# Weights of the experts in half pieces beside every second unit, and the row gathers placed behind the last grams

## The chip, the cores and the metric

The kernel runs on one core of one Trainium2 chip. The metric is the device time of one execution in microseconds. A core has the engines PE (TensorE), DVE (VectorE), ACT (ScalarE), POOL (GpSimd) and SP (SyncE); transfers run on 16 DMA engines. SP and POOL issue transfers, each on a queue of its own.

## The reference

Two stages follow each other. The first is a linear attention with a decaying state over 4 batches, 8 heads, 768 steps and a head size of 48. The second assigns each of the 3072 rows that come out (384 wide) to one of 8 experts with room for 384 rows each, by the order of all gate logits, and sends it through that expert's two matrices.

```python
for t in range(S):
    cur = einsum('bhd,bhe->bhde', u * kt, vt)
    y[:, :, t] = einsum('bhd,bhde->bhe', rt, state + cur)
    state = wt[..., None] * state + einsum('bhd,bhe->bhde', kt, vt)
x = y.transpose(0, 2, 1, 3).reshape(3072, 384)
for idx in argsort(-(x @ w_gate).flatten()):
    tok, e = idx // 8, idx % 8
    if assigned[tok] < 0 and counts[e] < 384:
        assigned[tok] = e; counts[e] += 1
for e in range(8):
    out[assigned == e] = maximum(x[assigned == e] @ w1[e], 0) @ w2[e]
```

Everything is float32 outside; w1 is 8 x 384 x 1024 and w2 is 8 x 1024 x 384, some 1.57 MB for each matrix of an expert.

## The kernel before

**Attention.** The steps are cut into 6 chunks of 128, and a chunk of one batch is a unit: 24 units, u = 0 to 23, chunk by chunk. For each unit SP loads r, k, v and w (192 KB each, rows of 192 bytes) into the tiles `kr`, `vv`, `ww`, of which there are two sets, so that a chunk's loads have to wait for the work of two chunks before. PE makes a cumulative sum of log w (`CUM`, tile `cps`), ACT and DVE turn it into factors, `MUL` on DVE scales k and r (`krs`), PE transposes (`T0`, `T1`) and makes the state product (`U`), the products with the state (`IA`), the grams (`G`, into `gps`) and the outputs (`Y0`, `Y1`, into `yps`). POOL makes r times k times u (`RK`, `RKU`) and from its sums the diagonal product (`DG`, tile `mm`), which DVE fills with the masked grams (`MS0`, `MS1`, line 557). The rows of a chunk go to a scratch tensor `x_scratch` in DRAM as bf16, and the gate logits are made beside it.

**Routing.** The first 20 tiles of rows decide early which 256 rows each expert gets in a first block (`Deal.early`, token list `tok1`, line 890). The rest is settled in rounds that run beside the first block, and gives a second block of 128 rows for each expert (`tok2`).

**Experts.** `Experts.block` goes through the experts: POOL gathers 128 rows by the token list (`gather`, line 1076), PE transposes them (line 1087), multiplies with w1 (`up`, line 1117), ACT or DVE take the positive part (`Fhs`), PE multiplies with w2 (`down`, line 1148), and POOL scatters the 128 output rows (line 1168). The first block has two gathers and two scatters for each expert, the second one.

**Weights.** Each matrix is one transfer on POOL's queue (lines 1024 and 1026), float32 in DRAM, bf16 in SBUF, where it takes 768 KB. Experts 0 to 3 have tiles of their own (`w1_0` to `w2_3`, shown as `w`); experts 4 to 7 go into the tiles `kr`, `vv` and `ww` of the last two chunks, once these are no longer used.

**What sets the order.** All operations are entered in a list with an engine, a cost and the operations that they come after. The attention part is laid out by a table of due times (`AT`, with a period of 4500 ns); `Line.merge` then puts everything else into the gaps, with a model of the clocks of all engines, and the instructions are written out in that order. An operation's `after` is a condition of the planner only: what waits at run time is what reads or writes the same data, or what needs the same one of eight semaphores of POOL's transfers. A weight's issue is entered as `Wi` on POOL and its transfer as `Wd` on the planner's DMA line. The first three come after the grams of units 16, 18 and 20 (`LOADS = 16`), and each also after an earlier transfer:

```python
by = [op["G", LOADS + 2 * len(loads)]] if len(loads) < 3 else []
a = line.add("Wi", (e, i), "POOL", 800, fn, after=begun + users + by, prio=-0.9)
begun = [a] if not loads else [a, loads[-1]]
```

POOL carries out its instructions in order, so that a transfer starts when POOL gets to it.

Of the kernel before, what the change touches and what calls it, by code (L numbers as in the profile page):

```python
# [24 lines left out]
F = 1024  # L25
# [645 lines left out]
FIRST = 256  # L671
# [349 lines left out]

def _weight_loads(nc, e, w1sb, w2sb, moe_w1, moe_w2):

    return [lambda: nc.gpsimd.dma_start(
                out=w1sb, in_=moe_w1[e].rearrange("(fc p) f -> p fc f", p=128)),
            lambda: nc.gpsimd.dma_start(
                out=w2sb, in_=moe_w2[e].rearrange("(fc p) d -> p fc d", p=128))]


class Experts:  # L1030
# [242 lines left out]

ROUNDS = N * (E - 1)
OWN = 4
LOADS = 16


def _constants(tc, const):
# [110 lines left out]
@with_exitstack  # L1390
def kernel(
    ctx: ExitStack,
    tc: tile.TileContext,
    r: bass.AP,
    k: bass.AP,
    v: bass.AP,
    w: bass.AP,
    u: bass.AP,
    moe_w_gate: bass.AP,
    moe_w1: bass.AP,  # L1400
    moe_w2: bass.AP,
    out: bass.AP,
):
    nc = tc.nc
    x_dram = nc.dram_tensor("x_scratch", (N, DX), BF16, kind="Internal").ap()

    cp = ctx.enter_context(tc.tile_pool(name="consts", bufs=1))
    keep = ctx.enter_context(tc.tile_pool(name="keep", bufs=1))
    inp = ctx.enter_context(tc.tile_pool(name="inputs", bufs=1))

    def const(name, shape, dtype=FP32):
        return cp.tile(shape, dtype, name=name, tag=name)

    negl = keep.tile([128, NTILE, E], FP32, name="negl", tag="negl")
    tok1 = keep.tile([128, FIRST * E // 128], I32, name="tok1", tag="tok1")
    tok2 = keep.tile([128, NTILE - FIRST * E // 128], I32, name="tok2", tag="tok2")
    a1 = keep.tile([128, NTILE, E], BF16, name="a1", tag="a1")
    flag = keep.tile([1, 1], I32, name="flag", tag="flag")
    q = keep.tile([E, 1], FP32, name="q", tag="q")
    weights = [(keep.tile([128, 3, F], BF16, name=f"w1_{e}", tag=f"w1_{e}"),  # L1420
                keep.tile([128, F // 128, DX], BF16, name=f"w2_{e}", tag=f"w2_{e}"))
               for e in range(OWN)]

    with ExitStack() as work, tc.manual_schedule():
        nc.scalar.preload_act_table_set("natural_log_exp_and_others")
        consts, later = _constants(tc, const)
        sb = work.enter_context(tc.tile_pool(name="work", bufs=1))
        def psum(name):
            return tc.tile_pool(name=name, bufs=1, space=bass.MemoryType.PSUM,
                                side="right" if "_c" in name else "left")  # L1430
        ps = work.enter_context(psum("psum"))
        wide = psum("psum_c")
        pc = wide.__enter__()
        stores = []
        line, ins, (Cps, Tps, Gps, Yps) = _attention(
            tc, inp, sb, ps, pc, r, k, v, w, u, moe_w_gate, x_dram, negl, consts, stores)
        op = line.op
        fixed = line.plan(lambda o: o.u * PERIOD + AT[o.name])
        assert fixed, "the keys lead to a deadlock"
        fixed = [x for x in fixed if x[1].prio is None]  # L1440


        last = NU - 1
        for c in range(NCH - 2, NCH):
            kr, vv, ww = (t[c % 2].bitcast(BF16) for t in ins)
            flat = kr.rearrange("p b x n -> p (b x n)"), vv.rearrange("p b n -> p (b n)"), \
                ww.rearrange("p b n -> p (b n)")
            for a in ((flat[0][:, :3 * F], flat[0][:, 3 * F:]), (flat[1], flat[2])):
                weights.append((a[0].rearrange("p (k f) -> p k f", k=3),
                                a[1].rearrange("p (k d) -> p k d", d=DX)))  # L1450
        loaded, loads = [], []
        begun = []
        for e in range(E):
            users = []
            if e >= OWN:
                c = NCH - 2 + (e - OWN) // 2
                for uu in range(c * B, c * B + B):
                    users += [op[x, uu] for x in ("MUL", "RK", "U", "Y1", "SUB")]
                    if ("WS", uu) in op:
                        users.append(op["WS", uu])  # L1460
            both = []
            for i, fn in enumerate(_weight_loads(nc, e, *weights[e], moe_w1, moe_w2)):
                by = [op["G", LOADS + 2 * len(loads)]] if len(loads) < 3 else []
                a = line.add("Wi", (e, i), "POOL", 800, fn, after=begun + users + by, prio=-0.9)
                begun = [a] if not loads else [a, loads[-1]]
                loads.append(line.add("Wd", (e, i), "DMA", 3500, lambda: None, after=[a],
                                      lag=1900, prio=-0.3))
                both.append(loads[-1])
            loaded.append(both)

        built = []
        for i, (engine, ns, fn) in enumerate(later):
            built = [line.add("X", i, engine, ns, fn, after=built, prio=0.5)]

        line.pools.update(B=4, D=2, FXG=Experts.XG, FXE=Experts.XE, FHS=Experts.HS,
                          FOS=Experts.OS)
        views = {"T": list(Tps), "D": [Yps[:, 0], Yps[:, 1]],
                 "B": [None, None] + Gps}

        def bank(pool, key):  # L1480
            i = line.slot[key]
            if views[pool][i] is None:

                wide.__exit__(None, None, None)
                new = work.enter_context(psum("psum_c2"))
                views[pool][:2] = [new.tile([128, 512], FP32, name=f"cps{x}", tag=f"cps{x}")
                                   for x in range(2)]
            return views[pool][i]
        deal = Deal(nc, line, bank, sb, consts, negl, "D", 20 * 16)
        deal.flag = flag  # L1490
        zero = deal.step("POOL", 200, lambda: nc.gpsimd.memset(a1[:, EARLY:], 0.0))
        deal.prio = -2
        first = deal.early(tok1, a1, op["LF", EARLY - 1], zero, *built)
        deal.prio = -1
        end = deal.round(q, DEPTHS[0], EARLY, deal.early_worst, op["LF", last])
        for depth in DEPTHS[1:]:
            end = deal.round(q, depth, None, (), end)
        second = deal.settle(q, tok2, a1, CAP - FIRST, end)

        ex = Experts(tc, line, bank, sb, consts, x_dram, weights, out, "F")  # L1500

        gets = ex.block(tok1, FIRST, loaded, 0, False, first,
                        *[op["Ls", c * B + B - 1] for c in range(NCH - 1)],
                        apart=lambda: stores[NCH - 1:])
        store = op["Ls", last].fn

        def apart():
            store()
            for got in gets:
                tc.declare_no_dep(stores[-1].ins, got.ins, reason="rows of other units")  # L1510
        op["Ls", last].fn = apart
        ex.block(tok2, CAP - FIRST, loaded, 1000, True, second, op["Ls", last])

        cs, gs, ys = [op["MUL", last]], [op["MS0", last], op["MS1", last]], [op["XB", last]]
        done = line.merge(fixed, {"B": [cs, cs, gs, gs], "D": [ys, ys]})
        assert done, "no order of all operations"
        for _, o in done:
            o.fn()
            o.last = line.last


    more = nc.values_load(flag[0:1, 0:1], min_val=0, max_val=2 * E)
    with tc.If(more > 0):
        tok = keep.tile([128, NTILE], I32, name="tok", tag="tok")
        with ExitStack() as a:
            sb = a.enter_context(tc.tile_pool(name="b_sb", bufs=1))
            ps = a.enter_context(tc.tile_pool(name="b_ps", bufs=1,
                                              space=bass.MemoryType.PSUM))
            line = Direct()
            banks = [ps.tile([128, 512], FP32, name=f"b{i}", tag=f"b{i}") for i in range(6)]  # L1530
            deal = Deal(nc, line, lambda pool, key: banks[line.slot[key]], sb, consts, negl,
                        "E", NTILE * NTILE)
            with tc.For_i(0, ROUNDS):
                deal.round(q, 8)
            deal.settle(q, tok, None, CAP)
        with ExitStack() as a:
            _experts(tc, a, x_dram, weights, out, tok, consts, "gx")
# [30 lines left out]
```

## Time and profile before

| | |
|---|---|
| median of 6 runs | 271.14 us (268.67 to 272.63) |
| profiled execution | 270.35 us, of which the span 268.4 us |
| PE busy | 217.8 us (81% of the span) |
| DVE, ACT, POOL busy | 143.6, 131.3, 148.6 us |
| share of the DMA engines: SP's queue, POOL's queue | 40.3%, 38.1% |
| moved by SP's and POOL's queue | 21.84 and 19.66 MB |
| mean granted clock of PE | 0.932 |

Bytes are counted at the destination, so that a weight counts with its bf16 size. The page gives the busy share in 40 slices of the span, and the chain of waits follows the work that ended last back from the end. A line of a timeline has start and duration in us, the engine, the line of the kernel, the operation, the tile written and those read, and a count; what stands in brackets is the idle time before it and what ended it. "issue" is time in which an engine waited for nothing that the profile shows. A row for a stretch of time has its length, the busy time and count of PE, of PE's weight loads, of DVE, ACT and POOL, and then PE's clock, the DMA share and GB/s. A DMA share can be a little over 1, where packets of one engine overlap.

### The profile page before, as it was taken

The page shows a single profiled execution, that of the slowest core. Times are in us where ns is not written, and L with a number is a line of the kernel's source. Part 1 is how long each engine was busy: PE and PEld are TensorE (multiplying, and loading weights), DVE is VectorE, ACT ScalarE, POOL GpSimd, SP SyncE. Part 2 cuts the span into 40 slices and gives each one's busy share as a digit, 9 for nine tenths or more (in the row PEclk, how much of TensorE's full clock was granted, in tenths as well). Part 3 has the DMA queues.
Part 4 walks back from the last instruction along what each step waited for, and adds up shares of the span by engine and source line. Part 5 has one row for each costly group of instructions (what it writes and reads, how often), then busy time and mean ns, then how long its engine had stood idle before and what let it go on. Part 6 is the DMA issues. An engine that isn't in the chain of part 4 may idle for free.

```text
span 268.4 us, 10437 instructions
## 1 busy us (share of the span) xinstructions
PE 217.8 (81%) x4469; PEld 161.7 (60%) x4469; DVE 143.6 (54%) x440; ACT 131.3 (49%) x248; POOL 148.6 (55%) x180
## 2 busy tenths in 40 slices
PE   2389997989998999776778481999899997968980
PEld 0266875777786677565566370767566875735850
DVE  6747676476675577546178770256555670114440
ACT  2156885675686667565434320355555664412210
POOL 7444685565756558566362548137765647572341
PEclk9999999999999999999689957579999999997995
DMA  7979798588878968979998993968999999232111
GB/s 146 187 140 173 136 178 200 114 174 186 161 153 179 176 126 190 199 144 179 185 203 104 179 180 79 172 150 184 175 221 203 205 195 257 96 104 76 59 64 66
DMA packets 118388, 42.24 MB, mean 157 GB/s; under 512 B 101440, under 2 KB 113728, under 8 KB 118336
## 3 DMA queue, kind: packets, MB, share of 16 engines
q1 hardware_dynamic: 104128, 21.84, 40.3%
q0 software_dynamic: 14208, 19.66, 38.1%
q8 instruction: 37, 0.61, 0.9%
q14 instruction: 15, 0.12, 0.2%
HBM read 46.61 MB, written 7.47 MB: 202 GB/s over the span
## 4 chain that ended last, share of the span: by engine, by line
PE 61%; DMA 9%; issue 9%; DVE 8%; POOL 4%; another core or an unknown queue 3%; SPq 2%; ACT 1%; POOLq 0%; DVEq 0%
PE yps L320 11%; PE tps L478 7%; PE gps L320 6%; PE tps L320 6%; PE cps L1117 6%; PE gps L1148 5%; PE gps L1117 5%; PE cps L320 4%; PE cps L1148 4%; DMA vv<-in_moe_w_dram 4%; DMA kr<-in_r_dram 3%; PE tps L590 2%; DMA u_bc<-in_u_dram 2%; POOL rku L457 2%
## 5 line engine op out<-in xcount | busy, mean ns | idle before, releaser
L466 POOL TENSOR_TENSOR mm<-diag,dd 128x512 f32<-128x512 f32 x24 | 25.2, 1048 | 54.0 <-DVE dd L461 26.4
L484 ACT COPY krT<-tps 112x512 f32<-112x512 f32 x48 | 28.1, 586 | 23.3 <-PE tps L478 20.1
L1168 POOL DMA_INDIRECT out_dram<-Fos,tok x24 | 24.1, 1003 | 24.5 <-DVE Fos L1158 13.7
L1076 POOL DMA_INDIRECT Fxg<-x_scratch,tok x24 | 23.5, 977 | 21.9 <-PE tps L1087 12.7
L557 DVE COPY_PREDICATED mm<-mask,gps 128x256 f32<-128x256 uint8 x48 | 18.7, 441 | 28.5 <-PE gps L320 14.1
L478 PE MATMUL tps<-ident,krs 128*112 128x128 f32 x192 | 31.8, 292 | 1.4 <-ACT row L604 0.8
L320 PE MATMUL cps<-ww,negut 128*128 128x384 f32 x48 | 24.0, 585 | 11.0 <-issue 5.4
L478 PEld LDWEIGHTS tps<-ident,krs 128*112 128x112 f32 x192 | 22.8, 141 | 12.4 <-issue 6.6
L453 POOL TENSOR_TENSOR rku<-kr 128x384 f32<-128x384 f32 x24 | 24.1, 1004 | 7.4 <-DMA kr<-in_r_dram 7.4
L320 PE MATMUL yps<-mm,vv 64*48 64x64 f32 x768 | 19.9, 232 | 9.4 <-DVE mm L557 6.2
L457 POOL TENSOR_TENSOR rku<-rku,u_bc 128x384 f32<-128x384 f32 x24 | 24.1, 1003 | 2.8 <-DMA u_bc<-in_u_dram 2.8
L320 PEld LDWEIGHTS yps<-mm,vv 64*48 64x48 f32 x768 | 14.6, 125 | 17.8 <-DVE mm L557 10.7
L1148 PEld LDWEIGHTS <-Fhs 128*128 128x128 bf16 x192 | 17.8, 100 | 11.9 <-issue 2.9
L578 ACT COPY xf<-yps 128x512 f32<-128x512 f32 x24 | 14.0, 582 | 21.7 <-PE yps L320 21.6
L447 DVE TENSOR_TENSOR krs<-kr,cps 128x768 f32<-128x768 f32 x24 | 22.7, 946 | 2.5 <-ACT cps L442 1.6
L320 PE MATMUL yps<-krT,sm 48*48 48x64 f32 x384 | 21.8, 230 | 1.6 <-issue 1.5
L320 PE MATMUL yps<-krT,st 48*48 48x64 f32 x384 | 21.6, 230 | 0.3 <-issue 0.3
L442 ACT ACTIVATE cps<-cps 128x768 f32<-128x768 f32 x24 | 19.3, 804 | 4.8 <-DVE cps L438 4.8
L1134 ACT ACTIVATE Fhs<-gps 128x512 bf16<-128x512 f32 x20 | 12.0, 598 | 15.5 <-PE gps L1117 9.4
L1117 PEld LDWEIGHTS <-w 128*128 128x128 bf16 x192 | 15.7, 103 | 6.3 <-issue 4.2
L1134 ACT ACTIVATE Fhs<-cps 128x512 bf16<-128x512 f32 x20 | 11.8, 597 | 15.1 <-PE cps L1117 11.6
L320 PE MATMUL gps<-krT 48*64 48x64 f32 x768 | 17.9, 229 | 1.1 <-issue 1.1
(200 smaller groups left out, 468.6 us busy)
## 6 DMA issues: line engine op xcount, KB each, us to landing
w<-in_moe_w_dram POOLq DMA_DIRECT2D x8, 768.0 KB
ww<-in_w_dram SPq DMA_DIRECT2D x24, 192.0 KB, 3.9
kr<-in_k_dram SPq DMA_DIRECT2D x24, 192.0 KB, 3.9
kr<-in_r_dram SPq DMA_DIRECT2D x24, 192.0 KB, 4.1
vv<-in_v_dram SPq DMA_DIRECT2D x24, 192.0 KB, 4.0
kr<-in_moe_w_dram POOLq DMA_DIRECT2D x4, 768.0 KB
x_scratch<-row SPq DMA_DIRECT2D x7, 384.0 KB, 5.2
vv<-in_moe_w_dram POOLq DMA_DIRECT2D x2, 768.0 KB
```

Of the source, the lines that this page charges most:

```text
L320: ln.last = nc.tensor.matmul(*a, **kw)
L447: fn=lambda u=u, kr=kr, b=b: nc.vector.tensor_tensor(out=KR[slot(("kr", u))][:, :, :, :D], in0=kr[:, b].rearrange("t x (h d) -> t x h d", ...
L453: fn=lambda u=u, kr=kr, b=b: nc.gpsimd.tensor_tensor(out=P[slot(("p", u))], in0=kr[:, b, 0, :], in1=kr[:, b, 1, :], op=ALU.mult))
L457: fn=lambda u=u: nc.gpsimd.tensor_tensor(out=P[slot(("p", u))], in0=P[slot(("p", u))], in1=u_bc, op=ALU.mult))
L466: fn=lambda u=u: nc.gpsimd.tensor_tensor(out=M[slot(("m", u))], in0=_free(diag, [0, 2], [0, NPAIR], [1, 64]), in1=_free(Dg[slot(("dg", u)) ...
L478: ln.last = nc.tensor.transpose(t[:112, at:at + 128], pair_of(s[:, x], j), ident)
L484: nc.scalar.copy(out=KRT[slot(("krt", u))][:112, 2 * half:2 * half + 2].rearrange("p j x t -> p (j x t)"), in_=Tps[slot(("t", u, half))][: ...
L1076: got = nc.gpsimd.indirect_dma_start(out=self.xg[slot[xg[1]]], out_offset=None, in_=self.x_dram, in_offset=bass.IndirectOffsetOnAxis(ap=to ...
L1117: nc.tensor.matmul(self.bank("B", b[1])[:, i * size:(i + 1) * size], lhsT=w1sb[:, k, f8 * 128:(f8 + 1) * 128], rhs=xv()[:, k], start=(k == ...
L1134: nc.scalar.activation(out=to, in_=of, func=AF.Relu)
L1148: nc.tensor.matmul(self.bank("B", b[1])[:, :DX], lhsT=hv()[:, f8, h * 128:(h + 1) * 128], rhs=w2sb[:, f8, :], start=(f8 == 0), stop=(f8 == ...
L1168: put = nc.gpsimd.indirect_dma_start(out=self.out, out_offset=bass.IndirectOffsetOnAxis(ap=tok[:, j:j + 1], axis=0), in_=self.os[slot[o[1] ...
```

## The change

Each matrix is now brought in two halves: w1 by its columns, w2 by its blocks of rows. There are 32 issues of 384 KB on POOL's queue in place of 16 of 768 KB. The n-th comes after the grams of unit 4 + 2n, at most of unit 23 (`LOADS = 4`); from the eleventh on it also comes after the transfer of three before it. An expert's multiplications come after the second half of its matrix in the planner. The gathers of the first block get one more condition in the planner, the grams of the last unit. After these edits the planner lays out all operations anew; up to the logits of the last chunk the order on PE is the same as before.

```diff
 def _weight_loads(nc, e, w1sb, w2sb, moe_w1, moe_w2):
-    return [lambda: nc.gpsimd.dma_start(
-                out=w1sb, in_=moe_w1[e].rearrange("(fc p) f -> p fc f", p=128)),
-            lambda: nc.gpsimd.dma_start(
-                out=w2sb, in_=moe_w2[e].rearrange("(fc p) d -> p fc d", p=128))]
+    w1 = moe_w1[e].rearrange("(fc p) f -> p fc f", p=128)
+    w2 = moe_w2[e].rearrange("(fc p) d -> p fc d", p=128)
+    f, k = F // 2, F // 256
+    return [lambda to=to, of=of: nc.gpsimd.dma_start(out=to, in_=of)
+            for to, of in ((w1sb[:, :, :f], w1[:, :, :f]), (w1sb[:, :, f:], w1[:, :, f:]),
+                           (w2sb[:, :k], w2[:, :k]), (w2sb[:, k:], w2[:, k:]))]
...
-LOADS = 16
+LOADS = 4
...
             for i, fn in enumerate(_weight_loads(nc, e, *weights[e], moe_w1, moe_w2)):
-                by = [op["G", LOADS + 2 * len(loads)]] if len(loads) < 3 else []
+                n = len(loads)
+                by = [op["G", min(LOADS + 2 * n, last)]]
                 a = line.add("Wi", (e, i), "POOL", 800, fn, after=begun + users + by, prio=-0.9)
-                begun = [a] if not loads else [a, loads[-1]]
-                loads.append(line.add("Wd", (e, i), "DMA", 3500, lambda: None, after=[a],
+                begun = [a] if LOADS + 2 * n < last else [a, loads[n - 2]]
+                loads.append(line.add("Wd", (e, i), "DMA", 1750, lambda: None, after=[a],
                                       lag=1900, prio=-0.3))
-                both.append(loads[-1])
+                both += [loads[-1]] * (i % 2)
             loaded.append(both)
...
-        gets = ex.block(tok1, FIRST, loaded, 0, False, first,
+        gets = ex.block(tok1, FIRST, loaded, 0, False, first, op["G", last],
                         *[op["Ls", c * B + B - 1] for c in range(NCH - 1)],
                         apart=lambda: stores[NCH - 1:])
```

## The prediction

> **What bounds the kernel now.** I read the page first, then the chain of waits, then the timelines of PE and POOL, then stretches of time. The page's second part shows two stages with different limits.
>
> ```profile
> PE   2389997989998999776778481999899997968980
> ...
> PEclk9999999999999999999689957579999999997995
> DMA  7979798588878968979998993968999999232111
> ```
>
> A slice is 6.71 us. Up to slice 15 PE is nearly full and the DMA engines are at about 0.8. From slice 16 on (107 us) the DMA share goes to 0.9 and more while PE falls to 0.4 to 0.8. From slice 28 to 33 both are full, and then the DMA falls quiet and PE alone works to the end. The chain names what was late at the three seams:
>
> ```profile
> 127.17 8.96 DMA kr<-in_r_dram
> ...
> 159.65 7.93 another core or an unknown queue
> ...
> 212.24 11.34 DMA vv<-in_moe_w_dram
> ```
>
> The first is an input load of unit 22 that landed 9 us after its issue, the second a wait of VectorE in the last unit, the third the w1 of expert 7, which PE needed at 221.9 and got at 223.63. What attention loses to the weights is read from PE's timeline: one cumulative-sum matmul opens each unit.
>
> ```profile
> 72.35 0.87 PE L320 MATMUL cps<-ww,negut 128*128 128x384 f32 x2
> ...
> 87.96 0.87 PE L320 MATMUL cps<-ww,negut 128*128 128x384 f32 x2
> 94.56 0.87 PE L320 MATMUL cps<-ww,negut 128*128 128x384 f32 x2
> ...
> 110.31 0.87 PE L320 MATMUL cps<-ww,negut 128*128 128x384 f32 x2
> 117.72 0.87 PE L320 MATMUL cps<-ww,negut 128*128 128x384 f32 x2
> ...
> 140.71 0.91 PE L320 MATMUL cps<-ww,negut 128*128 128x384 f32 x2
> ```
>
> These are units 12, 15, 16, 19, 20 and 23. Unit 12 to 15 takes 15.61 us, 16 to 19 takes 15.75, 20 to 23 takes 22.99: 7.4 us lost. The step from 19 to 20 takes 7.41 against 6.60 from 15 to 16: another 0.8. Together 8.2 us. POOL issues the weights in its own order:
>
> ```profile
> 105.26 0.96 POOL L1024 DMA_DIRECT2D w<-in_moe_w_dram  x1
> ...
> 119.44 0.95 POOL L1026 DMA_DIRECT2D w<-in_moe_w_dram  x1
> ...
> 128.42 0.80 POOL L1024 DMA_DIRECT2D w<-in_moe_w_dram  x1
> ```
>
> **The change, part by part.** *Where the pieces go.* The planner's "after" is only a rank: in the list of instructions of the changed kernel no weight issue and no gather waits for a gram. POOL reaches each in its order. Ten halves (five old pieces) now stand before the gathers: after the diagonal product of unit 4, then by units 7, 9, 11, 12, 15, 16, 19, 20 and 23. On the clock of before these are about 39, 54, 65, 76, 83, 99, 105, 122, 128 and 157 us. Before, six whole pieces stood there (the three above, 141.35, 149.53, 150.33). So three halves come at the times of the three whole pieces that cost 8.2 us, six come earlier, and one old piece in all moves behind the gathers.
>
> *Removed late.* A whole piece by itself: the first, at 105.26. Unit 18 to 20 (103.09 to 117.72) takes 14.63 us, unit 14 to 16 (80.89 to 94.56) took 13.67: 0.96 us. The next two, 9 us apart, have the rest: 3.6 us each. So a half costs between nothing and 1.8 us; the nearest row is the piece by itself, 0.48 for a half. The three late ones can cost between nothing and 4.1 (half of 8.2); I take 2.0, nearer to three times 0.48 than to the half, since what is late only counts beyond what the loads have in hand. Gain 8.2 - 2.0 = 6.2.
>
> *Added early.* Six halves between 39 and 99 us, beside input loads:
>
> ```profile
> 50.00:72.00 22.00, 20.71 (x622) 15.87 (x622) 14.06 (x35) 15.08 (x29) 13.76 (x17) 1.00 0.82 166
> ...
> 116.00:127.00 11.00, 8.88 (x255) 6.96 (x254) 7.04 (x17) 7.05 (x13) 7.14 (x9) 1.00 1.01 168
> 170.00:172.00 2.00, 2.00 (x34) 1.61 (x32) 0.26 (x1) 1.01 (x3) 0.00 (x0) 0.50 1.11 211
> ```
>
> The last two columns are DMA share and GB/s. Weights alone pass at about 205 GB/s (170 to 176 us), so a whole piece of 786 KB takes 3.84 us and a half 1.92. Early there are 0.18 x 22 = 4 us to spare in a chunk of four units, and two halves take 3.84: the engines become full but not overfull, and each half lengthens the way of the loads beside it (landing takes 4 us in the median). At 0.48 each: 2.9 us. Bounds nothing and 6 x 1.8 = 10.8. Attention in sum: -6.2 + 2.9 = -3.3. Bounds: -8.2 with halves that cost nothing, and -8.2 + 4.1 + 10.8 = +6.7. POOL's own time for ten issues against six is hidden: it waits up to 2.7 us for VectorE's sums in each unit; without that cover four more issues would be 3.6 us.
>
> *The tail.* After the gathers 22 halves (11 old pieces) have to pass, before ten. The DMA queue is busy without a break from 190 to 228 us, so the 3.84 us of one piece are added at its end. Then the order. Before, the pieces of expert 3 follow the six gathers directly (166.10 and 166.91), they are through at 178, and the next waits behind three gathers that need PE's transposes:
>
> ```profile
> 178.00:180.00 2.00, 2.00 (x20) 1.22 (x18) 1.02 (x4) 1.30 (x4) 0.25 (x1) 1.00 0.04 11
> 180.00:182.00 2.00, 1.93 (x18) 1.46 (x17) 1.83 (x9) 1.47 (x4) 1.69 (x3) 1.00 0.19 48
> ...
> 180.70 0.83 POOL L1024 DMA_DIRECT2D kr<-in_moe_w_dram  x1
> ```
>
> After, three halves follow the gathers (5.8 us of work, not 7.7) and the next stands behind four gathers, 1.3 us later: the gap grows by 1.9 + 1.3 = 3.2. The last half thus lands 3.84 + 3.2 = 7.0 us later against the start of the tail. Of this PE gets back 1.5: the last down projection needs its second half only after four of 16 matmuls (eight take 1.30 us, so four 0.65), and 15 up matmuls of the second block stand before it (twelve take 0.67, so 15 take 0.8). Tail +5.5. Bounds: -1.5, if the added piece fits the gap; +10, if the queue runs dry, since w1 of expert 6 now stands behind the scatter of expert 4 (before at 214.25) instead of before it (issued at 203.55). 22 issues instead of ten cost POOL up to 12 x 0.9 = 11 us; it idles some 33 of the 80 us from 158 to 238, which hides them.
>
> [...]
>
> *The gathers.* They stand in the same place on POOL and wait for the same token list, so VectorE's wait of 7.9 us beside the six gathers stays. I cost this part at nothing.
>
> **Sum.** -3.3 + 5.5 = +2.2 us. The profiled execution took 270.35 us (span 268.4, 1.95 around it), 0.8 under the median of 271.14; I add the sum to the median: 273.3.
>
> **Rivals.** *The early halves cost more* (the side is the same, the size is not): at 1.2 us for each of the nine, attention is at +2.6 and the time 279. For it: units 20 to 23, and PE's stalls on issue, which grow from 1.1 to 2.3 us beside weights. Against: half the bytes at nearly twice the distance. *The queue runs dry in the tail:* -3.3 + 10 = 278. *The tail gives nothing back,* the rival on the other side: the added piece goes into the idle 5 us from 178 on, and smaller transfers feed PE sooner. Then -3.3 - 1.5 = -4.8 and 266.3; it decides if the next half is issued before the queue is empty. For it: the gap is there. Against: that half stands behind one more gather. *The gathers do come after the grams,* so the change does what its words say: the wait of VectorE (to 167.62) would end with the grams (162.66), 5.0 less, and the gathers and all weights behind them would start 1.9 later: 273.3 - 3.1 = 270.2. Against: no wait in the list.
>
> **How the numbers follow.** A measurement of this kernel tells about 1% from no change, that is 268.4 and 273.9. My forecast has 0.42, with a range of its own of 270 to 277: of it 0.02 faster, 0.21 same, 0.19 slower. Dear early halves 0.20 and a dry queue 0.08, all slower. A tail that costs nothing 0.20, all faster. Gathers after the grams 0.10: 0.04 faster, 0.06 same. Together faster 0.26, same 0.27, slower 0.47. The range from 264.5 to 281 takes in the time of every rival and leaves out the bounds of the attention term.
>
> **What would show it.** Right: units 20 to 23 within 18 us; the steps of units 4 to 16 longer by 2 to 4 us in all; the gathers' first issue 2 to 5 us earlier than 158.74; PE waiting for weights of experts 6 and 7, with w1 of expert 7 landing about 68 to 74 us after that issue (before 64.9). Wrong: a first gather at or after 158.7 (the attention term), no wait for weights in the tail (the tail term), or a VectorE wait beside the gathers that is gone.

## The result and the profile after

The changed kernel took 277.45 us in the median of 20 runs (271.9 to 283.53), the kernel before 270.68 us in 46 runs (266.63 to 276.77). The ratio is 1.0192, 95% interval 1.0146 to 1.0238: slower, on the side that the forecast gave most chance, 4 us over its 273.3. The ratio leaves out the slower executions of each kernel, those more than 1.5% above its fastest, and the profiled execution of the changed kernel, 279.7 us with a span of 277.9, is one of these, while that of the kernel before, 270.35 us with a span of 268.4, is not. A second pair of traces, 271.39 against 267.53 us, comes further down.

The second part of the page, PE, granted clock and DMA share in slices of 6.95 us:

```profile
PE   2089987798898897889696966489999977789960
...
PEclk9999999779999999799978685599999979799996
DMA  7958789778989999998992341785999999923120
```

Before, the clock row was full up to slice 18. Now it falls to 7 in slices 7 and 8 and again in slice 16; PE is below 9 in most of the first sixteen slices, and the DMA engines have little to do in slices 21 to 24 (146 to 174 us), ahead of the gathers and beside the first ones. The openings of units 4, 16, 20 and 23 in PE's timeline:

```profile
28.78 0.87 PE L320 MATMUL cps<-ww,negut 128*128 128x384 f32 x2
...
103.23 0.87 PE L320 MATMUL cps<-ww,negut 128*128 128x384 f32 x2
...
128.78 0.87 PE L320 MATMUL cps<-ww,negut 128*128 128x384 f32 x2
...
148.92 0.91 PE L320 MATMUL cps<-ww,negut 128*128 128x384 f32 x2
```

Units 4 to 16 take 74.45 us (before 94.56 - 28.41 = 66.15), units 20 to 23 take 20.14 (22.99). POOL's timeline has the first half and the first gather:

```profile
39.48 0.96 POOL L1027 DMA_DIRECT2D w<-in_moe_w_dram  x1
...
168.26 1.06 POOL L1078 DMA_INDIRECT Fxg<-x_scratch,tok  x1 [0.32 <-DVE tok L890]
```

The gather comes 9.5 us later than before (158.74), and from it to the end of the span there are 109.64 us (109.66). So in this pair of traces all of the loss lies in attention, and the tail (all that comes from the first gather on) is unchanged. The chain of waits names what stands there now:

```profile
109.62 2.70 issue
136.23 2.53 issue
169.15 7.90 another core or an unknown queue
...
217.12 7.66 DMA ww<-in_moe_w_dram
...
232.50 5.73 DMA Fxg<-x_scratch,tok
```

Stalls on issue in attention, the same wait of VectorE as before (7.93), then waits for weights and for rows in the tail.

**Where attention lost it.** The stretch of units 4 to 16, before:

```profile
28.41:94.56 66.15, 60.97 (x1858) 46.98 (x1856) 42.15 (x102) 45.13 (x85) 41.95 (x49) 1.00 0.82 165
```

and after:

```profile
28.78:103.23 74.45, 64.95 (x1858) 49.64 (x1856) 42.30 (x102) 45.34 (x85) 45.94 (x54) 0.95 0.89 168
```

The numbers behind the length are PE, PEld, VectorE, ScalarE, POOL, the clock, the DMA share and GB/s. PE's longest waits in the stretch after the change (total, times, longest):

```profile
PE gps L320 <- issue: 4.1, 5, 1.2
PE tps L320 <- issue: 4.0, 3, 2.3
```

The same 1858 matmuls are busy 4.0 us longer at a mean clock of 0.95, and PE is idle 9.5 us instead of 5.2, most of it on "issue". What these stalls are, the counts between their ends show:

```profile
38.00:43.38 5.38, 4.27 (x128) 3.26 (x128) 3.46 (x8) 3.28 (x7) 4.29 (x6) 1.00 0.78 133
...
66.10:76.59 10.49, 9.54 (x254) 7.09 (x255) 6.73 (x16) 5.62 (x11) 6.84 (x9) 1.00 1.01 191
76.59:86.44 9.85, 9.01 (x255) 6.66 (x255) 4.97 (x13) 6.75 (x13) 6.42 (x8) 1.00 0.93 161
86.44:95.92 9.48, 7.69 (x255) 6.15 (x256) 5.61 (x13) 6.02 (x12) 6.71 (x9) 1.00 0.97 192
```

From one stall's end to the next PE executes 128 matmuls and 128 weight loads, or twice that: the stalls sit at multiples of 256 instructions. The queue for instructions moves 37 packets, 0.61 MB in all, 16 KB each. In windows of 0.1 us from 47.7, 110.0 and 136.5 us the DMA view has:

```profile
q8 instruction: 1, 0.02, 60.1%
...
q8 instruction: 1, 0.02, 58.4%
...
q8 instruction: 1, 0.02, 59.9%
```

A packet counts here with its whole time in the window in which it starts, so each of these occupies one engine for some 0.96 us (0.6 x 16 engines x 0.1). PE goes on at 50.09, 112.32 and 138.75, 2.2 to 2.4 us after the packet began. The reading, an estimate from these times and counts: PE waits for its next 256 instructions, they come in one such packet of 16 KB, and the packet starts late.

What the engines carry just before shows what is in the way. POOL's queue (q0, the weights) and SP's queue (q1, the inputs) from 42 to 45, from 45 to 48 and from 107 to 110 us:

```profile
q0 software_dynamic: 363, 0.36, 76.3%
q1 hardware_dynamic: 781, 0.15, 33.8%
...
q1 hardware_dynamic: 2262, 0.64, 90.1%
...
q0 software_dynamic: 319, 0.32, 74.1%
q1 hardware_dynamic: 528, 0.10, 27.2%
```

While a half passes, it has three quarters of the engines' time and the inputs have a third or less; then the inputs catch up with the engines full. The packets at 110.0 and 136.5 us start as a half ends, the one at 47.7 some 2.5 us behind a half, among the late inputs.

The rest is the clock behind the stalls:

```profile
47.83:50.09 2.26, 0.00 (x0) 0.00 (x0) 0.14 (x1) 0.58 (x1) 0.00 (x0) 1.00 1.05 230
...
51.54:54.96 3.42, 3.42 (x77) 3.33 (x77) 0.43 (x2) 2.18 (x4) 1.69 (x2) 0.50 0.66 129
54.96:58.38 3.42, 3.42 (x49) 2.35 (x50) 1.19 (x4) 1.23 (x3) 2.23 (x3) 0.50 0.32 46
...
113.00:116.41 3.41, 3.41 (x88) 2.82 (x86) 2.63 (x7) 2.55 (x5) 1.43 (x2) 0.50 1.07 212
```

After a stall of 2.26 us the clock is at one half for 6.84 us, after one of 2.70 for 3.41. PE's 4.0 us more of busy time for the same matmuls come with the 6.84 us.

### The profile page after: what moved, and what is told of

Read it like the earlier page. It is cut to its first block, busy times and chain, and to the rows that moved or that the text cites. A ratio compares the mean times of both kernels' runs of the same rounds, so it can differ in the third digit from the quotient of the medians.

```text
span 277.9 us, 10445 instructions
## 1 busy us (share of the span) xinstructions
PE 221.7 (80%) x4469; PEld 165.3 (59%) x4469; DVE 145.6 (52%) x440; ACT 131.5 (47%) x248; POOL 159.8 (58%) x196
## 4 chain that ended last, share of the span: by engine, by line
PE 64%; issue 9%; DVE 8%; DMA 7%; ACT 3%; another core or an unknown queue 3%; POOL 2%; POOLq 0%; ACTq 0%; DVEq 0%
PE yps L320 11%; PE tps L478 8%; PE gps L320 7%; PE cps L320 6%; PE tps L320 6%; PE gps L1119 6%; PE cps L1119 5%; PE cps L1150 5%; PE gps L1150 4%; DMA ww<-in_moe_w_dram 3%; DMA ww<-in_w_dram 2%; PE tps L590 2%; DMA Fxg<-x_scratch,tok 2%; DVE Dohl L870 1%
## 5 line engine op out<-in xcount | busy, mean ns | idle before, releaser
L478 PE MATMUL tps<-ident,krs 128*112 128x128 f32 x192 | 32.7, 298 | 1.4 <-ACT row L604 0.8
L478 PEld LDWEIGHTS tps<-ident,krs 128*112 128x112 f32 x192 | 23.3, 143 | 12.3 <-issue 6.3
L320 PE MATMUL yps<-mm,vv 64*48 64x64 f32 x768 | 20.8, 241 | 9.6 <-DVE mm L557 6.1
L320 PEld LDWEIGHTS yps<-mm,vv 64*48 64x48 f32 x768 | 15.5, 132 | 18.2 <-DVE mm L557 10.8
L320 PE MATMUL yps<-krT,sm 48*48 48x64 f32 x384 | 22.5, 238 | 0.3 <-issue 0.2
L320 PE MATMUL gps<-krT 48*64 48x64 f32 x768 | 19.3, 233 | 4.2 <-issue 4.2
L320 PE MATMUL yps<-krT,st 48*48 48x64 f32 x384 | 22.4, 238 | 0.1
L442 ACT ACTIVATE cps<-cps 128x768 f32<-128x768 f32 x24 | 19.3, 804 | 5.3 <-DVE cps L438 5.3
L320 PEld LDWEIGHTS gps<-krT 48*64 48x64 f32 x768 | 16.2, 148 | 5.3 <-issue 5.2
L320 PE MATMUL gps<-vv,krs 64*48 64x48 f32 x768 | 15.6, 221 | 4.1 <-issue 4.1
```

Source lines behind the costliest of these rows:

```text
L320: ln.last = nc.tensor.matmul(*a, **kw)
L442: fn=lambda: nc.scalar.activation(out=Cps[:, 128:896], in_=Cps[:, 128:896], func=AF.Exp))
L478: ln.last = nc.tensor.transpose(t[:112, at:at + 128], pair_of(s[:, x], j), ident)
```

## The experiments

Theory A: in attention the DMA engines have no room beside the inputs, so a weight transfer there makes instructions and inputs late, whatever its shape; PE stalls and its clock falls. Rivals: B, the issues in POOL's order cost; C, the cut itself costs.

The table has all traces; "4-16" and "16-23" are the times between unit openings, "tail" runs from the first gather to the end of the span. Chips differ, so rows are compared within a chip where there are such rows: the first two rows; x1 to x4; the two rows "again"; x5 to x8; z1 and z2. Each row has one trace, and the times between openings vary by some us from trace to trace of one kernel (4-16: 66.15 and 67.32 before, 74.45 and 69.75 changed).

| kernel | old pieces ahead of the gathers | 4-16 | 16-23 | first gather | tail | time, median (before beside it) |
|---|---|---|---|---|---|---|
| before | 6 | 66.15 | 46.15 | 158.74 | 109.66 | 270.68 |
| changed | 5 (halves) | 74.45 | 45.69 | 168.26 | 109.64 | 277.45 |
| x1, old places | 7 (halves) | 67.47 | 45.36 | 163.03 | 108.17 | 271.71 (270.0) |
| x2, early | 5 | 73.68 | 43.89 | 162.34 | 108.96 | 276.12 (270.0) |
| x3, gathers only | 7 | 65.02 | 43.63 | 154.59 | 108.01 | 267.68 (270.0) |
| x4, none early | 0 | 66.17 | 39.49 | 151.49 | 126.81 | 281.81 (270.0) |
| changed again | 5 (halves) | 69.75 | 45.45 | 160.87 | 108.63 | 273.49 (268.53) |
| before again | 6 | 67.32 | 43.82 | 157.54 | 108.06 | 268.53 |
| x5, late | 6 | 66.14 | 39.50 | 155.88 | 96.72 | 254.63 (251.91) |
| x6, bytes out | 2 (halves) | 61.46 | 42.26 | 149.91 | 111.79 | 271.15 (251.91) |
| x7, late | 6 (halves) | 65.57 | 40.86 | 154.68 | 99.12 | 255.48 (251.91) |
| x8, late | 3 | 62.77 | 38.99 | 151.01 | 106.19 | 263.03 (251.91) |
| z1, as x5 | 6 | 67.09 | 42.14 | 156.79 | 95.21 | 253.37 (255.21) |
| z2, as x7 | 6 (halves) | 67.55 | 41.95 | 157.45 | 99.15 | 256.44 (255.21) |

**x1: the cut at the old places.** In the changed kernel:

```
-LOADS = 4
+LOADS = 16
-by = [op["G", min(LOADS + 2 * n, last)]]
+by = [op["G", LOADS + 2 * (n // 2)]] if n < 6 else []
-begun = [a] if LOADS + 2 * n < last else [a, loads[n - 2]]
+begun = [a] if n < 2 or n % 2 == 0 else [a, loads[n - 2]]
```

> The cut alone: halves, two at a time, at the places where whole pieces stood, with the gathers' edit, which here puts one more old piece (the w1 of expert 3) ahead of the gathers. No half before unit 16. Theory A (bytes beside the early units: PE's inputs and instructions land late, PE stalls and its clock falls): units 4 to 16 take 66 to 67 us as before, first gather at 158 to 162, time 270 to 273, the same as the kernel with the gathers' edit alone. Rival B (the number of issues in POOL's order costs, not the bytes): 14 issues stand before the gathers against 7, all from unit 16 on, so units 16 to 23 grow by 4 to 6 us. Rival C (the cut itself costs: twice the packets for w1, shorter rows): time at least 3 us over the kernel with the gathers' edit alone, most of it after the gathers, where 18 halves pass.

Units 4 to 16 are where they were. Against the kernel before the ratio is 1.0128 (1.0 to 1.0256). Units 16 to 23 are 1.7 us longer than in x3, not the 4 to 6 of B. The median is 4.0 us over that of x3, with ranges that overlap (269.64 to 273.28 and 264.47 to 271.68). In the traces the difference lies ahead of the gathers (163.03 against 154.59), not in the tail, so C falls in the form that put most of it behind the gathers. A price of the cut ahead of them, of up to these 4 us, remains possible.

**x2: the early places, whole pieces.** In the kernel before (a third line, which lets the early pieces go without an earlier transfer, is left out here):

```
-by = [op["G", LOADS + 2 * len(loads)]] if len(loads) < 3 else []
+by = [op["G", min(LOADS + 4 * len(loads), last)]]            # LOADS = 4
```

> The early timing alone: the same five old pieces before the gathers, but whole, by units 4, 8, 12, 16 and 20, and the gathers as in the kernel before. Theory A (bytes): units 4 to 16 grow by about as much as in the changed kernel (8.3 us; 6 to 9), the first gather comes at 165 to 169, time 276 to 279. Rival B (issues): half as many issues, so half the growth, 3 to 5 us. Rival C (cut): units 4 to 16 as before within 2 us, first gather at 156 to 160, time 267 to 271.

```profile
27.16:100.84 73.68, 65.29 (x1859) 49.91 (x1855) 42.03 (x102) 45.17 (x85) 44.64 (x52) 0.93 0.92 175
```

Three whole pieces by units 4, 8 and 12 lengthen units 4 to 16 by 73.68 - 66.17 = 7.5 us against x4, which ran on the same chip with no weights there. In the changed kernel five of the six early halves are issued within these units (the sixth at 104.95, 1.7 us after unit 16 opened) and brought 8.3: three issues do about what five did. The clock is 0.93 and PE's stalls on issue are 7.9 us. The median is 6.1 us over the kernel before, with ranges that overlap (273.14 to 278.61 and 265.31 to 275.18), and this is nearly the whole loss of the change (6.8). So the early place alone is enough for it, and the cut is not needed. Whether the cut adds to it is not told by this.

**x3: the gathers' edit.** Only `op["G", last]` is added in the kernel before.

> The gathers' edit alone. It waits for nothing, but moves the planner's rank of the gathers, and so one more whole piece ahead of them and each later piece one place ahead in POOL's order. As predicted on record (costs nothing): 268 to 273. Rival (one more piece before the gathers costs up to 3.6 us in the last unit as the late ones do, and gives back up to 3.84 behind): first gather up to 4 us later, tail up to 4 us shorter, time the same within 1%. Rival D (the edit is what makes the changed kernel slow): 275 or more.

The ratio is 0.9987 (0.9915 to 1.0059): no difference that this shows. The seventh piece ahead of the gathers neither cost nor gave. VectorE's wait beside the gathers stays (5.77 and 0.92 us).

**x4: nothing early.** In the kernel before each piece gets `by = [op["G", last]]`.

> No weights before the last unit's gathers: the floor of attention beside its own inputs. All 16 whole pieces follow the gathers. Expected by theory A: units 4 to 16 as before (66 to 67 us; only one early step changes, none had weights), units 16 to 23 shorter by the 8.2 us that the prediction read off, first gather at 148 to 152. The tail has six more old pieces to pass, 6 x 3.84 = 23 us, less the gaps in which its transfers stand still (5 to 10 us): 123 to 128 us from the first gather to the end instead of 109.7, time 274 to 281. If instead the tail grows by less than 10 us, weights before the gathers are not needed at all and the time falls under 265. If units 16 to 23 do not get shorter, the weights were not what slowed them before.

This gives both prices, of weights beside attention and of weights left to the tail. Attention's floor for units 16 to 23:

```profile
94.39:116.43 22.04, 20.34 (x622) 15.68 (x620) 14.08 (x34) 14.85 (x29) 13.75 (x17) 1.00 0.81 165
116.43:133.88 17.45, 14.82 (x467) 11.45 (x464) 12.88 (x28) 10.81 (x21) 11.65 (x15) 1.00 0.60 127
```

39.49 us at full clock: by this one trace the weights cost the kernel before 6.7 and 4.3 us there in its two traces, which are from other chips, and x3, on this chip, 4.1; none has the 8.2. The tail is 126.81, that is 17 us for six missing pieces, or 2.9 each. With five, six and seven pieces ahead it is 108 to 109.7 in the seven other traces of the chips on which the kernel before takes 268 to 271 us.

**x5 to x8** ran on another chip, on which the kernel before takes 251.91 us and has no trace; their traces are compared among themselves. x5 and x8 start from the kernel before, x6 and x7 from the changed one.

> The same six whole pieces before the gathers as in the kernel before, but all of them beside units 20, 21 and 22, two each; nothing else changes. In the kernel without any early weights the DMA engines stand nearly idle from 132 us to the gathers, since the inputs are all in. Theory A (a piece costs attention about what it takes on the DMA engines as long as inputs pass, 2.5 to 3 us, and nothing after; the tail needs five to six pieces ahead): units 4 to 16 in 65 to 67 us, 16 to 20 in 22 to 24, first gather at 151 to 155, 108 to 110 from there to the end, time 262 to 267. Rival E (the place does not matter: what the pieces cost early they cost late, by the gathers that stand in the same queue behind 23 us of weights): the gathers are issued early but their rows land late, time 269 to 274.

```
+LOADS = 20
+by = [op["G", min(LOADS + len(loads) // 2, last)]]
+begun = [a] if len(loads) < 6 else [a, loads[-1]]
```

The middle of attention came to the floor as expected (88.2 us for units 4 to 20), but the first gather came 20.1 us after the opening of unit 23, against 17.3 to 19.3 in the two kernels before and after, and the ratio is 1.0109 (1.001 to 1.0208). The gain that A forecast did not come. POOL issued only two of the six pieces, at 129.06 and 130.01, before unit 23 opened at 135.79; the other four came from 136.43 to 147.47. What they cost there, and whether E is right about the rows, is open without a trace of the kernel before on this chip.

> The changed kernel with its six early halves replaced by six small transfers (128 rows of 64 bytes into a tile that nothing reads) at the same places in POOL's order; the weights themselves start with four single halves at units 16, 18, 20 and 22, and three old pieces more come after the gathers. Theory A (bytes): units 4 to 16 back to 65.5 to 67.5 us (the changed kernel 74.45), PE's stalls on issue there under 5 us (8.5), the granted clock 0.99 to 1.00 (0.95). Rival B (the issues): units 4 to 16 at 71 us or more. The tail has 14 old pieces to pass: 113 to 120 us from the first gather.

```
-LOADS = 4
+LOADS = 16
...
+for n in range(6):
+    line.add("Wb", n, "POOL", 800, lambda n=n: nc.gpsimd.dma_start(
+        out=bit[:, n], in_=moe_w1[0, :128, :32]), after=[op["G", 4 + 2 * n]], prio=-0.9)
```

The stretch of units 4 to 16, and PE's waits in it:

```profile
26.84:88.30 61.46, 60.07 (x1858) 46.43 (x1856) 41.85 (x102) 44.93 (x85) 44.61 (x54) 1.00 0.88 178
```

```profile
PE gps L320 <- issue: 0.8, 1, 0.8
PE yps L320 <- issue: 0.2, 1, 0.2
```

POOL has the 54 instructions of the changed kernel there (before 49), and the stretch is the shortest of the four on this chip (61.46 against 62.77 to 66.14), with 1.0 us of stalls and a full clock. B falls: without their bytes the early issues cost nothing here. The changed kernel itself was not run on this chip, so its loss here is not known.

> Twelve halves at the places of the six whole pieces of the run with all early weights beside units 20 to 22: the cut, where no input load is beside it, with the gathers as in the kernel before. If the cut costs nothing but POOL's time: the same as with whole pieces within 1%, the first gather up to 3 us later for six more issues. If the cut costs by itself (more packets, more issues in the tail, 20 against 10): 2 to 5 us more, as between the two runs with the pieces from unit 16 on (271.7 and 267.7).

> Three whole pieces, beside units 20, 21 and 22, the rest behind the gathers: what the tail asks of the weights ahead of it. With none ahead the tail took 126.8 us, with five to seven 108 to 109.7. By theory A attention is at its floor, first gather 151 to 153. If the tail is bound by the transfers (3.84 us for each missing piece): tail 116 to 119, time 270 to 273. If it is bound by PE with three ahead already: tail 109 to 111, time 262 to 266. The two pieces that the prediction on record moved between attention and tail would cost 3.8 each by the first and nothing by the second.

x7 is x5 with the halves' code and `by = [op["G", min(LOADS + n // 4, last)]]`; x8 is x5 with `by = [op["G", LOADS + len(loads) if len(loads) < 3 else last]]` and the condition of `begun` from the third piece on. Halves: tail 2.4 us longer, time 0.3% more. Three pieces ahead instead of six: tail 106.19 instead of 96.72, 3.2 us for each. This is near the 3.84 of the first alternative, a tail bound by the transfers. On the chips of the kind of the first the tail did not change between five and seven pieces ahead; fewer than five were tried there only with none.

**The pair again.** Both kernels, unaltered, on a chip like the first:

> The changed kernel once more, unaltered. The last four runs were made on a chip on which the kernel before takes 252 us instead of 270, and on which VectorE did not wait beside the six gathers (1.4 us instead of 8.0); the run with the bytes of the early halves left out took 61.5 us for units 4 to 16 there, without a changed kernel beside it. Theory A (bytes): units 4 to 16 are 5 to 9 us longer than in the kernel before on the same chip, with stalls on issue and, behind some of them, a granted clock of 0.5; from the first gather on no longer than before by more than 3 us; time 1.5% to 3.5% over the kernel before. Rival F (the loss is one of the first chip alone, where the DMA engines were fuller): units 4 to 16 within 3 us, time within 1%.

> The kernel before once more, unaltered, for a trace from the same chip as the changed kernel's. If it is the quick chip: first gather at 151 to 155, VectorE's wait beside the gathers under 2 us, tail 96 to 99. If it is one like the first: first gather at 155 to 160, VectorE's wait 8 us, tail 108 to 110. Units 4 to 16 at 62 to 66 in either.

273.49 against 268.53 us, 1.8% (four runs from 270.29 to 276.28, seven from 265.22 to 271.91). Attention loses 3.3 us (160.87 against 157.54), of it 2.4 in units 4 to 16; the tail 0.6. That stretch grew by less than the 5 to 9 us that A expected, and by less than the 3 that F allowed; the time grew by more than F allowed. Five stalls of more than 0.5 us on issue are there in the changed kernel, but the longest is 1.72 us, and only one stretch of half clock followed, of 3.41 us. The size of the loss thus differs from execution to execution, and so does the time (271.9 to 283.53): the trace with 8.3 us is one of 279.7 us, this one is of 271.39.

**z1 and z2**: x5 and x7 once more, on a second quick chip.

> Six whole pieces beside units 20 to 22 once more. On the quick chip this was 1.1% over the kernel before, with attention at its floor (units 4 to 20 in 88 us) and the first gather at 155.9, 20 us after the last unit opened, not 18. On a chip like the first, where the tail has a floor of about 108 us: first gather at 152 to 156, from there 107 to 110, time 262 to 266 against 268 to 270, 1.5% to 2.5% faster. If POOL's queue with six pieces ahead of the gathers makes the last unit as much longer as the middle units get shorter: the same within 1%. On the quick chip again: 1% slower.

> The same with twelve halves. If the changed kernel's tail lost nothing because half pieces between the gathers break up POOL's runs of gathers and scatters, behind which VectorE waits (5.9 us at 235 us before the change, 13.8 and 6.8 us in the second trace of the kernel before): VectorE's waits in the tail, the one in the last unit apart, are under 2 us here too, PE waits for weights or rows for 3 to 6 us instead, and the tail is 107 to 110 us. Time within 1% of the run with whole pieces, up to 1% above it for more issues.

Ratios 1.0051 (0.9969 to 1.0133) and 1.0129 (0.9954 to 1.0305): no difference from the kernel before that these show, and no version that beats it. The medians with halves lie over those with whole pieces in all three pairs, by 4.0 (x1 over x3), 0.9 (x7 over x5) and 3.1 us (z2 over z1), so that the cut may have a part in the loss; how much of the 6.8 us is not told. The tail is again longer with halves (99.15 against 95.21), with PE waiting 3.3 us for a w1 in a `kr` tile. z2 says nothing on VectorE's waits beside gathers: on these two chips no kernel has them.

## Why the prediction was right on the side and wrong in its terms

That the side came out is luck. Attention was forecast to gain 3.3 us and lost 9.5 and 3.3 in the two pairs; the tail was forecast to lose 5.5 and lost nothing and 0.6. Two errors of opposite sign gave a sum on the right side.

*The gathers' edit at nothing:* right. No wait came of it, and x3 alone makes no measurable difference; that it moves one more piece ahead by rank was not seen.

*POOL's issues hidden:* right (x6).

*Early halves, +2.9 at 0.48 each:* too low for the first pair, met in the second. The five that are issued in units 4 to 16 bring 8.3 us and 2.4, that is 1.7 and 0.5 for each; whole pieces 2.5 (x2). The price came from a row where the clock stayed full and one piece passed alone. "Four us to spare in a chunk" is true of bytes; the engines are busy 0.82 on the mean, but while a half passes it has three quarters of them (76.3% and 74.1%), inputs and instruction packets come late, and the clock (0.95 on the mean in the first pair) makes it dearer. The rival of dear early halves had the mechanism. Its 279 us is near the 277.45 measured, but its sum is not: its +2.6 for attention stands against 9.5 and 3.3, and its tail term did not come.

*Late halves, -6.2:* the step that failed, in both pairs. It took 8.2 us as the price of the three whole pieces and 2.0 for three halves. The 8.2 was read against units 12 to 15, but units 20 to 23 take 17.45 us even with no weights (x4), not 15.61. The floor of x4 makes the price 6.7 and 4.3, and the changed kernel is 6.2 and 6.0 over the same floor: 45.69 and 45.45 against 39.49. Four halves pass beside these units, since the sixth of the early ones is issued after unit 16 opens; the sum had 2.0 + 0.48 = 2.5 for the four, with 4.1 + 1.8 = 5.9 as their upper bound. Four halves in place of three whole pieces, a third fewer bytes, gained 0.5 us in one pair and lost 1.6 in the other. A stall is not always halved with the piece: the one ahead of unit 22, at the same instruction in each, is 2.25 and 2.47 us before, 2.53 and 1.08 after, 0.59 with no weights (x4). That each half is one more chance to meet a packet is argued from this and not shown.

*Tail, +5.5:* measured 0.0 and +0.6. The waits came as foreseen, in the first trace after:

```profile
PE tps L1089 <- DMA Fxg<-x_scratch,tok: 2.4, 2, 1.8
PE cps L1150 <- DMA ww<-in_moe_w_dram: 1.9, 2, 1.6
PE cps L1150 <- DMA kr<-in_moe_w_dram: 1.0, 1, 1.0
```

5.3 us for weights and rows (5.9 in the second trace), before 1.7 and none. They were for experts 5 and 6 and the second block's rows; w1 of expert 7 was in by 238.05, where a wait of POOL on it ends, 69.8 us after the first gather, as forecast. What was missed is that other waits went. PE's idle time in the tail is 21.3 and 21.9 us before, 22.2 and 23.3 after. Before, VectorE is held in the second block; the first and the second trace of that kernel:

```profile
241.01 0.69 DVE L1132 TENSOR_SCALAR Fhs<-gps 128x512 bf16<-128x512 f32 x1 [5.88 <-remote]
```

```profile
230.92 0.36 DVE L1099 COPY Fxe<-tps 128x384 bf16<-128x384 bf16 x1 [13.81 <-remote]
238.12 1.29 DVE L1132 TENSOR_SCALAR Fhs<-gps 128x512 bf16<-128x512 f32 x2 [6.84 <-remote]
```

while POOL issues gathers and scatters one after the other; in the second trace PE waits 4.2 and 1.6 us for these two. In the changed kernel VectorE has no such wait behind the last unit in either trace. The halves as such do not do it. x1, all in halves with seven old pieces ahead, has the longest such wait of all:

```profile
237.75 0.36 DVE L1101 COPY Fxe<-tps 128x384 bf16<-128x384 bf16 x1 [15.35 <-remote]
```

x3, whole pieces with seven ahead, has 14.74 and 6.17 us; x2, whole pieces with five ahead, and x4, with none, have no such wait. So on these chips the waits are in the traces with six or seven pieces ahead and not in those with five or none; why is open. And the tail has no more to gain from a sixth or seventh piece (x1, x3: 108 us), so it loses little with the fifth.

The forecast let POOL's idle time hide the additional issues in the tail. With ten more transfers there, x7 and z2 have tails 2.4 and 3.9 us longer than x5 and z1 with whole pieces; how much of it is the issues is not shown.

Of the signs named ahead, the VectorE wait in the last unit, PE's waits for weights (of experts 5 and 6, not 6 and 7) and the landing of expert 7's w1 came; the steps of units 4 to 16 grew by 8.3 and 2.4 us where 2 to 4 were named; units 20 to 23 within 18 us (20.14 and 20.27) and an earlier gather did not, and the second is the sign that was named for a wrong attention term.

## What to carry to other kernels

That bytes fit is not enough for a prefetch: in units 4 to 16 the DMA engines were busy 0.82 on the mean, and three whole pieces cost 7.5 us there (x2), five halves 8.3 and 2.4. Look for stalls on "issue" at a fixed count of instructions (256 here), and for a clock below 1.00 behind them (0.95 and 0.93 here), before putting transfers there. A prefetch that was moved to where the inputs are already in left the stretch before at its floor (units 4 to 20: 88.2 us in x5 and, on another chip, 88.2 in x4), but did not make the kernel faster (x5, ratio 1.0109): both what it costs there and what it gains behind have to be measured, since the tail had a floor of its own (108.0 to 109.7 us with five to seven pieces ahead, on the chips like the first). Price a transfer from a run without any, not from the difference between two stretches with different work.

## What the runs showed of the hardware that was not expected

*Half clock followed some short stalls, in steps of 3.41 us.* Half-clock stretches of 3.41 and 6.84 us follow stalls of 2.70 and 2.26 us in the changed kernel, one of 10.24 us, three steps, goes with a stall of 2.26 in x2, and one of 3.41 follows a stall of 1.72 in the second trace of the changed kernel. In the second trace of the kernel before a stall of 2.47 us had none:

```profile
127.94:130.41 2.47, 0.00 (x1) 0.00 (x1) 1.16 (x2) 0.16 (x1) 1.17 (x2) 1.00 1.26 203
130.41:134.00 3.59, 3.28 (x119) 2.57 (x123) 1.12 (x3) 2.49 (x5) 3.11 (x4) 1.00 0.98 166
```

These four stalls of 1.7 to 2.7 us went with half clock, and the one of 2.47 us did not. No run shows what decides this.

*Chips differ in one wait.* On the chips where the kernel before takes 268 to 271 us, VectorE's copy beside the six gathers was held in each of the eight traces, in six of them until the last gather was issued (7.2 to 8.0 us). On the two chips where it takes 252 to 255 us the same copy started between them in all six traces, as in x5:

```profile
158.11 0.77 DVE L557 COPY_PREDICATED mm<-mask,gps 128x256 f32<-128x256 uint8 x2 [1.41 <-PE gps L320]
```

POOL's gathers take the same there (973 ns in the mean in x5, 977 in the kernel before). What makes the chips differ is open. The changed kernel was not run on such a chip, nor the late pieces on one like the first; what the change does on the one and the late places on the other is open.
